# Attention and two expert layers on one core: first weight splits on GpSimd, a condition around the repeated body, and new queue orders

## The chip, the core and the metric

One core of one Trainium2 chip runs the whole program. The metric is device time in microseconds (us) of one execution, smaller is better. The kernel before takes 460.74 us, the median of three runs (460.49 to 464.29).

## What is computed

Three layers follow one another:

```python
q_rot, k_rot = rotate(q), rotate(k)             # 2 batches, 8 heads, 576 tokens, 64 wide
attn = softmax(q_rot @ k_rot.T / sqrt(64))
x = (attn @ v)                                  # -> (1152 tokens, 512)
h = x @ w_in; x = (h * sigmoid(1.702 * h)) @ w_out       # 512 -> 2048 -> 512
e = argmax(x @ w_gate); g = softmax(x @ w_gate)[e]       # one of 8 experts per token
out = g * (relu(x @ w1[e]) @ w2[e])             # 512 -> 1024 -> 512, at most 288 tokens an expert
```

The weights w_in and w_out arrive as 8-byte floats and are made into 4-byte ones on the chip. To keep the accuracy, each 4-byte operand of a large product is split into a high part that TensorE takes as it is and a low part, the rest, and three products (high by high, high by low, low by high) are summed.

## The kernel before, in words

**Attention** works on 8 pairs of heads. For one pair, nine tiles of 128 rows go through the same steps, each a method of `Attention`: `rope` and `start` (rotation of keys and queries, lines 434 and 436), `scores` (TensorE, lines 450 and 461), `least` (VectorE, 473), `exps` (ScalarE, 485), `turn` (transposes by TensorE, 501), `turned` (copies out of PSUM by ScalarE or VectorE, 382 and 383), `rest`, `sums`, `spread` and `placed` for the leftover rows and the row sums, `inverse` (538, 541), `weighted` (TensorE, 576), `divided` (580), and `halved`, which writes the high and low part of the result into `xt` (383 and 591). The function `plan` gives every step of every pair a time out of a table (`FIRST` for pair 0, `SECOND` for pair 1, `LAST` for pair 7, `ORDER` for the others; a unit is a ninth of a pair) and sorts them. `run` issues them in that order, and `pin` chains the instructions of each engine in it, so a table fixes the order of every engine's queue within attention, not the times themselves. `ENGINES` and `LAST_ENGINES` say which engine does a copy.

**The first layer** is `Experts.first`, called for 480, 384 and 288 tokens in turn. For each of 16 slices of the weights, `halves` splits a slice: ScalarE writes the high part (line 744), VectorE the low part (745), into a ring `hl` of four places. `hidden` multiplies (TensorE, 758), `gated` applies the gated function (ScalarE 793 and 794, VectorE 795), and `ffn` multiplies again two slices later (TensorE, 784). In the first call the slices are also made out of 8-byte numbers: `Weights.units` gives, for each slice, two loads (SyncE, 647) and two cuts of three VectorE instructions each (657, 658, 659). The first four slices (`EARLY`) are loaded and cut inside attention, as the events named `spare` of `plan`; the other twelve are issued by `get` and lie where the scheduler puts them. The scheduler also mixes the instructions of the first layer with the end of attention, where data and space allow it.

Space in SBUF is handed out pool by pool, like a stack. The ring `hl` lies where attention kept `turns`, `qk` and `warm` (pool `at_keys`), so its first write waits for the last pair's last scores.

**The second layer** is routed by `route` (rows are sent to a table in memory by GpSimd, 959), fetched by `gather` (1031, 1036), multiplied in `second` and `few`, and sent out by GpSimd (`send`, 1081). Items beyond the four fixed ones run in a loop with a trip count read on the chip; in these inputs there are none, so its body runs zero times:

```python
n = nc.values_load(self.etab[0:1, ITEMS:ITEMS + 1], min_val=4, max_val=ITEMS)
with tc.For_i(4, n, 1) as i:
```

Of the kernel before, what the change touches and what calls it, by code (L numbers as in the profile page):

```python
# [9 lines left out]
F32 = mybir.dt.float32  # L10
# [15 lines left out]
P = 128  # L26
# [19 lines left out]
    (-117.147, 0, 0, CUT, "vector"),  # L46
    (-104.32, 1, 0, P, "vector"),
    (-93.539, 0, CUT, WIDTH, "vector"),
    (-70.102, 1, P, 2 * P, "vector"),
    (-63.518, 1, 2 * P, WIDTH, "gpsimd"),  # L50
# [3 lines left out]
    "rope1": "vector",  # L54
    "t0": "scalar",
    "t1": "vector",
    "t2": "scalar",
    "t3": "vector",
# [4 lines left out]
    "t8": "scalar",  # L63
    "twice": "gpsimd",
    "rr0": "gpsimd",
    "rr1": "gpsimd",
# [4 lines left out]
    "rest_pick0": "scalar",  # L71
# [11 lines left out]
    "t2": "vector",  # L83
# [7 lines left out]
    "rr0": "scalar",  # L91
    "rr1": "scalar",
    "rest0": "vector",
    "rest1": "scalar",
    "sums0": "scalar",
    "sums1": "scalar",
    "rest_pick0": "vector",
    "rest_pick1": "vector",
    "sums_pick0": "scalar",
    "sums_pick1": "scalar",  # L100
    "hix0": "scalar",
    "hix1": "scalar",
    "lox0": "vector",
# [3 lines left out]
RING = 4  # L107
BANKS = 4
# [7 lines left out]
    "scores": (-5.379, 0.0, -5.357, 0.0, -6.652, -5.845, 0.0, -5.773, 0.0),  # L116
    "least": (-4.474, -4.977, -5.096, -5.338, -5.786, -4.946, -5.929, -4.499, -5.286),
    "exps": (-4.007, -2.826, -3.155, -4.498, -4.52, -4.577, -3.986, -3.964, -4.374),
    "turn": (1.18, -0.002, 1.073, 0.066, 0.278, 0.016, -1.338, -2.497, -3.627),
    "turned": (1.29, 1.428, 2.134, 0.802, 0.53, 0.02, 1.733, -2.198, -1.851),  # L120
    "twice": 2.069,
    "rest": (4.203, 7.954),
    "rest_placed": (4.344, 8.225),
    "inverse": (0.431, 5.697),
    "spread": (4.518, 7.776),
    "sums": (8.547, 11.796),
    "sums_placed": (8.668, 11.978),
    "weighted": ((5.82, 5.83, 6.247, 7.416, 7.558), (8.943, 9.276, 9.72, 11.863, 11.866)),
    "divided": (9.825, 12.617),
    "halved": ((10.838, 13.114), (14.097, 16.936)),  # L130
    "rope": (-14.244, -14.237, -11.208, -14.485, -14.198, -8.14),
    "load": (-23.726, -22.572),
    "load_v": -1.934,
    "spare": (58.904, 2.443),
}
FIRST = {
    "scores": (-73.792, 0.0, -59.267, 0.0, -30.868, -18.807, 0.0, -14.272, 0.0),
    "least": (-66.526, -68.104, -48.52, -41.921, -19.608, -13.489, -14.156, -13.209, -13.952),
    "exps": (-48.59, -64.421, -33.102, -36.449, -17.654, -10.259, -11.532, -11.371, -8.342),
    "turn": (-47.159, -45.687, -14.692, -22.644, -11.218, -8.976, -9.913, -7.426, -8.299),  # L140
    "turned": (-34.39, -24.662, -12.818, -6.58, -8.825, -5.338, -6.898, -5.868, -6.252),
    "twice": -11.395,
    "rest": (-10.966, 1.724),
    "rest_placed": (-7.234, 2.438),
    "inverse": (-4.857, 4.371),
    "spread": (3.041, 7.264),
    "sums": (4.504, 7.484),
    "sums_placed": (4.832, 8.961),
    "weighted": ((-2.669, -1.615, 2.832, 4.428, 5.729), (3.158, 4.024, 5.6, 10.857, 10.98)),
    "divided": (6.612, 11.82),  # L150
    "halved": ((8.342, 14.847), (13.13, 19.618)),
    "load_v": -73.006,
# [6 lines left out]
    "turned": (-0.511, -2.93, 2.06, 0.063, 0.948, 2.183, -0.623, 0.18, -0.429),  # L159
    "twice": -2.399,  # L160
    "rest": (3.666, 7.876),
    "rest_placed": (4.094, 8.323),
    "inverse": (-1.23, 5.28),
    "spread": (1.497, 6.761),
    "sums": (8.477, 10.839),
# [1082 lines left out]
```

## Time and profile before

| | us |
|---|---|
| median of 3 runs | 460.74 |
| the profiled execution | 461.19 |
| its span, first to last instruction | 459.4 |
| around the span | 1.8 |

In the profile, PE is the matmuls of TensorE, PEld its weight loads, DVE is VectorE, ACT ScalarE, POOL GpSimd, SP SyncE. A row of a table of windows gives the length of the stretch, then the busy time of each engine with its number of instructions in brackets. A line such as L758 is a line of the kernel. In a timeline the first number is the start, the second the time it took, and square brackets give the idle time before and what ended it. The granted clock of TensorE is 0.994 of 2.4 GHz over the span.

### The profile page before, as it was taken

How to read it: one execution, taken by the hardware profiler on the slowest of the kernel's cores; microseconds unless marked ns; L12 is line 12 of the kernel's file. 1: busy time of each engine (PE TensorE's matmuls, PEld its weight loads, DVE VectorE, ACT ScalarE, POOL GpSimd, SP SyncE). 2: the span in 40 equal slices, each digit the busy share in tenths (PEclk: the TensorE clock that was granted, in tenths of full speed). 3: DMA queues.
4: the chain of work that ended last, by engine and by line, in shares of the span. 5: the costliest groups of instructions: out<-in, count | busy, mean ns of one | idle time of the engine just before them, and what ended most of it. 6: DMA issues, size and time to landing. Idle time of an engine off the chain costs nothing.

```text
span 459.4 us, 9065 instructions
## 1 busy us (share of the span) xinstructions
PE 436.6 (95%) x3380; PEld 373.4 (81%) x3380; DVE 309.7 (67%) x693; ACT 266.0 (58%) x558; POOL 123.9 (27%) x130
## 2 busy tenths in 40 slices
PE   7899999999988999999999999999999999999991
PEld 3556666666565878788999999999999999999980
DVE  5866866677968889997355344457846697765670
ACT  1788888888858252445453445475566455464560
POOL 1589877983210000000000000000526033701020
PEclk9999999999999999999999999999999999999997
DMA  8614421331315756550011600001175446874510
GB/s 279 235 71 145 144 72 75 144 122 30 139 53 177 257 165 245 216 188 1 0 36 34 224 0 1 0 27 46 6 271 182 145 139 186 247 260 157 185 51 16
DMA packets 20319, 57.11 MB, mean 124 GB/s; under 512 B 3749, under 2 KB 5957, under 8 KB 20272
## 3 DMA queue, kind: packets, MB, share of 16 engines
q1 hardware_dynamic: 17584, 52.09, 33.4%
q0 software_dynamic: 1728, 3.62, 2.6%
q10 hardware_dynamic: 960, 0.79, 0.5%
q8 instruction: 28, 0.46, 0.4%
q14 instruction: 19, 0.16, 0.1%
HBM read 49.91 MB, written 6.66 MB: 123 GB/s over the span
## 4 chain that ended last, share of the span: by engine, by line
PE 57%; issue 15%; DVE 10%; DMA 9%; POOL 4%; ACT 3%; SPq 0%; POOLq 0%; DVEq 0%; ACTq 0%
PE h L758 18%; PE y L784 17%; PE t L576 7%; PE s L461 6%; PE t L501 5%; DMA slots<-entry,r_at 2%; DMA raw<-in_w_in 2%; DVE pp L473 2%; POOL slots L959 2%; PE tr L849 2%; POOL out L1081 2%; DVE wf L659 2%; PE s L450 2%; DMA ent<-slots 1%; DVE m L658 1%
## 5 line engine op out<-in xcount | busy, mean ns | idle before, releaser
L758 PE MATMUL h<-xt,hl 128*128 128x288 f32 (+3 forms) x864 | 159.9, 324 | 3.5 <-ACT hl L744 1.4
L758 PEld LDWEIGHTS h<-xt,hl 128*128 128x128 f32 x864 | 135.2, 188 | 11.2 <-ACT hl L744 2.4
L784 PE MATMUL y<-gh,hl 128*128 128x288 f32 (+3 forms) x576 | 123.9, 322 | 0.4 <-ACT gh L794 0.4
L745 DVE TENSOR_TENSOR hl<-wf,hl 128x1024 fp32r<-128x1024 f32 x72 | 87.9, 1224 | 51.3 <-ACT hl L744 51.2
L744 ACT ACTIVATE hl<-wf 128x1024 fp32r<-128x1024 f32 x72 | 76.1, 1059 | 49.6 <-DVE wf L659 26.1
L784 PEld LDWEIGHTS y<-gh,hl 128*128 128x128 f32 x576 | 94.9, 188 | 4.3 <-ACT gh L794 0.8
L784 PE MATMUL y<-gl,hl 128*128 128x288 f32 (+3 forms) x288 | 77.0, 321 | 0.0
L959 POOL DMA_INDIRECT slots<-entry,r_at x12 | 15.0, 1254 | 208.0 <-ACT hl L744 184.3
L793 ACT ACTIVATE g<-h 128x480 f32<-128x480 f32 (+2 forms) x48 | 23.2, 491 | 63.1 <-PE h L758 54.3
L473 DVE TENSOR_SCALAR_CACHE_REDUCE pp<-s 128x576 f32<-128x576 f32 x64 | 45.8, 754 | 16.2 <-PE s L461 15.8
L485 ACT ACTIVATE pp<-pp,nm 128x576 f32<-128x576 f32 x64 | 49.3, 771 | 12.5 <-DVE pp L473 11.8
L784 PEld LDWEIGHTS y<-gl,hl 128*128 128x128 f32 x288 | 50.9, 188 | 1.8
L795 DVE TENSOR_TENSOR gl<-g,gh 128x480 fp32r<-128x480 f32 (+2 forms) x48 | 26.5, 555 | 27.5 <-ACT gh L794 27.2
L434 POOL TENSOR_TENSOR qk<-qk,turns 128x640 f32<-128x640 f32 (+1 forms) x28 | 41.5, 1507 | 9.5 <-DMA qk<-in_qk 9.5
L461 PE MATMUL s<-qk 64*128 64x288 f32 x256 | 40.8, 421 | 3.1 <-DVE pp L473 1.4
L382 ACT ACTIVATE pt<-t 128x512 f32<-128x512 f32 (+1 forms) x65 | 32.8, 538 | 10.4 <-PE t L501 10.3
L576 PE MATMUL t<-pt,vr 128*64 128x288 f32 x256 | 38.3, 419 | 0.1
L501 PEld LDWEIGHTS t<-ident,pp 64*128 64x128 f32 x576 | 23.7, 138 | 16.2 <-issue 4.2
L501 PE MATMUL t<-ident,pp 64*128 64x64 f32 x576 | 28.8, 230 | 2.6 <-ACT pt L382 0.9
L461 PEld LDWEIGHTS s<-qk 64*128 64x128 f32 x256 | 24.0, 188 | 8.3 <-DVE pp L473 2.6
L576 PEld LDWEIGHTS t<-pt,vr 128*64 128x64 f32 x256 | 15.5, 136 | 13.4 <-issue 3.8
L794 ACT ACTIVATE gh<-g 128x480 fp32r<-128x480 f32 (+2 forms) x48 | 24.8, 525 | 1.1
(173 smaller groups left out, 473.6 us busy)
## 6 DMA issues: line engine op xcount, KB each, us to landing
wf<-in_w SPq DMA_DIRECT2D x32, 512.0 KB, 4.5
qk<-in_qk SPq DMA_DIRECT2D x14, 640.0 KB, 5.5
raw<-in_w_in SPq DMA_DIRECT2D x16, 512.0 KB, 4.4
raw<-in_w_out SPq DMA_DIRECT2D x16, 512.0 KB, 3.8
vr<-in_v SPq DMA_DIRECT2D x8, 320.0 KB, 5.0
x<-row SPq DMA_DIRECT2D x12, 192.0 KB, 2.1
out<-zero SPq DMA_DIRECT2D x9, 256.0 KB, 3.0
qk<-in_qk SPq DMA_DIRECT2D x1, 384.0 KB, 4.8
```

The source lines that it names most:

```text
L382: return e.activation(out=out, in_=x, func=AF.Copy)
L434: e.tensor_tensor(out=u, in0=u, in1=self.turns[:, k, ts], op=ALU.mult)
L461: nc.tensor.matmul(both[h][:, n, 0:HALF], q[hs, at:at + P], k[hs, key:key + HALF], start=True, stop=True)
L473: self.nc.vector.tensor_scalar(out=self.room(p, i).rearrange("p (n k) -> p n k", n=2), in0=self.open.pop(("s", p, i))[:, :, 0:HALF], scala ...
L485: self.nc.scalar.activation(out=x, in_=x, func=AF.Exp, scale=-1.0, bias=self.nm[p % 2][:, i:i + 1], accum_out=self.sum[p % 2][:, i:i + 1],)
L501: self.nc.tensor.transpose(banks[b][:, at:at + 64], x[bs], self.ident[bs, bs])
L576: self.nc.tensor.matmul(o[h * 64:h * 64 + 64], x, y, start=j < 2, stop=j > 7)
L744: nc.scalar.activation(out=hl[:, 0], in_=t, func=AF.Copy)
L745: self.last = nc.vector.tensor_tensor(out=hl[:, 1], in0=t, in1=hl[:, 0].bitcast(F32), op=ALU.subtract).ins
L758: self.nc.tensor.matmul(h, u, v, start=m == 0, stop=m == len(ops) - 1)
L784: nc.tensor.matmul(y[j][:, 0:w], u, v, start=f == LAG and m == 0, stop=f == n + LAG - 1 and m == 2)
L795: nc.vector.tensor_tensor(out=gl, in0=g, in1=gh.bitcast(F32), op=ALU.subtract)
```

## The change

1. **Tables and engines.** All five `START` times, every entry of `ORDER`, `FIRST`, `SECOND` and `LAST` and the pace of the early weights (`spare`) are new. In pair 1 both rotations go to GpSimd (the second was VectorE's). In pairs 0 to 6 the copies `t0`, `t2`, `t8` and `rest_pick0` go to VectorE, `t1`, `t3`, `twice`, `rr0` and `rr1` to ScalarE. In pair 7 `rr0` and `lox0` go to GpSimd, `rest1`, `sums1`, both `sums_pick` and both `hix` to VectorE, `t2`, `rest0` and both `rest_pick` to ScalarE.
2. **Space.** `turns` and the `qk` of the pairs that are not the last lie in a pool of their own, `at_odd`; `warm` moves to `at_sums`. The ring becomes two tiles of two places each. The first of them lies in the space of `at_odd`.
3. **Splits.** The first two slices are split by GpSimd, both parts, placed in its queue after its last instruction for pairs 0 to 6.
4. **Order.** The first VectorE instruction of every cut of the twelve later slices is put behind VectorE's last instruction of attention. It is an order within the queue, not a semaphore.
5. **Function table.** After the last `exps` a one-column Gelu on `warm` is issued on ScalarE.
6. **Loop.** The loop stands inside a condition, and its iterations are synchronised in another way.

```diff
     "rope0": "gpsimd",
-    "rope1": "vector",
+    "rope1": "gpsimd",
...
+FIRST_CUTS = 2
...
-    "spare": (58.904, 2.443),
+    "spare": (53.608, 3.254),
...
 LAST = {
...
-    "exps": (-2.224, -5.239, -3.759, -4.874, -3.323, -3.213, -2.722, -3.427, -3.232),
+    "exps": (2.776, -2.966, -2.927, -3.517, -2.774, 2.401, 6.256, 52.03, 36.27),
...
-    "halved": ((78.406, 94.851), (98.733, 141.7)),
+    "halved": ((174.91, 208.013), (237.477, 240.964)),
...
-        self.turns, = some(keys, 1, "turns", 2, WIDTH + 64)
-        self.qk = some(keys, 3, "qk", 4, WIDTH)
-        self.warm = keys.tile([P, 512], BF16, name="warm")
+        last = (B * NPAIR - 1) % 3
+        qk = {k: odd.tile([P, 4, WIDTH], F32, name=f"qk{k}") for k in range(3) if k != last}
+        self.turns, = some(odd, 1, "turns", 2, WIDTH + 64)
+        qk[last] = keys.tile([P, 4, WIDTH], F32, name=f"qk{last}")
+        self.qk = [qk[k] for k in range(3)]
+        self.warm = sums.tile([P, 512], BF16, name="warm")
...
+    def ready(self):
+        self.nc.scalar.activation(out=self.warm[:, 0:1], in_=self.warm[:, 1:2], func=AF.Gelu_apprx_sigmoid)
+
     def run(self, spare):
-        for _, _, f, args in plan(len(spare)):
+        events = plan(len(spare))
+        tail = max(k for k, e in enumerate(events) if e[2] == "exps")
+        for k, (_, _, f, args) in enumerate(events):
             self.pin((lambda: spare[args[0]]()) if f == "spare" else (lambda: getattr(self, f)(*args)))
+            if f != "spare" and f != "start" and args[0] < B * NPAIR - 1:
+                self.calm = dict(self.last)
+            if k == tail:
+                self.pin(self.ready)
...
-            v.tensor_scalar(out=m, in0=top, scalar1=3, scalar2=0x3FFFFFF8, op0=left, op1=both)
+            ins = v.tensor_scalar(out=m, in0=top, scalar1=3, scalar2=0x3FFFFFF8, op0=left, op1=both)
+            if not early:
+                self.tc.add_manual_dep(ins.ins, self.after[ins.ins.engine], self.order, reason="order")
...
-        self.ring = pool("hl", 1).tile([P, RING, 2, 2 * DM], F32R, name="hl")
+        rings = [pool(f"ring{i}", 1) for i in range(RING // 2)]
+        self.ring = [ring.tile([P, 2, 2, 2 * DM], F32R, name=f"hl{i}") for i, ring in enumerate(rings)]
...
     def halves(self, t):
         nc = self.nc
-        hl = self.ring[:, self.cuts % RING]
+        hl = self.slot(self.cuts)
         self.cuts += 1
+        if self.cuts <= FIRST_CUTS:
+            ins = nc.gpsimd.tensor_copy(out=hl[:, 0], in_=t)
+            self.tc.add_manual_dep(ins.ins, self.weights.calm[ins.ins.engine], self.weights.order, reason="order")
+            self.last = nc.gpsimd.tensor_tensor(out=hl[:, 1], in0=t, in1=hl[:, 0].bitcast(F32), op=ALU.subtract).ins
+            return hl
...
-        with tc.For_i(4, n, 1) as i:
+        with tc.If(n > 4, label="more"), tc.For_i(4, n, 1, iteration_sync="staggered") as i:
```

## Rows read from the trace of the kernel before

**Rows 1.** The page's first part: busy time, share of the span, instructions

```profile
PE 436.6 (95%) x3380; PEld 373.4 (81%) x3380; DVE 309.7 (67%) x693; ACT 266.0 (58%) x558; POOL 123.9 (27%) x130
```

**Rows 2.** Windows: the start of attention, and one pair in mid-attention

```profile
7.40:13.50 6.10, 3.84 (x35) 2.12 (x35) 4.25 (x13) 1.96 (x5) 3.40 (x4) 1.00 0.99 364
13.50:20.00 6.50, 5.71 (x51) 3.72 (x52) 6.07 (x13) 4.45 (x13) 4.36 (x4) 1.00 0.53 218
...
87.64:102.46 14.82, 14.70 (x169) 9.63 (x169) 9.82 (x27) 12.91 (x38) 12.20 (x15) 1.00 0.27 96
```

**Rows 3.** Windows: the end of attention and the first layer's first call

```profile
117.20:122.00 4.80, 4.29 (x34) 2.52 (x34) 4.66 (x11) 3.61 (x12) 0.56 (x1) 1.00 0.55 204
122.00:127.00 5.00, 4.51 (x49) 2.77 (x45) 4.93 (x14) 4.54 (x9) 1.22 (x2) 1.00 0.45 144
...
133.40:138.00 4.60, 3.86 (x62) 2.63 (x64) 4.08 (x10) 2.72 (x6) 0.00 (x0) 1.00 0.14 26
138.00:143.40 5.40, 4.43 (x40) 2.36 (x36) 3.59 (x9) 4.78 (x12) 0.52 (x1) 1.00 0.50 175
143.40:148.00 4.60, 3.42 (x15) 2.67 (x16) 4.53 (x9) 3.40 (x8) 0.00 (x0) 1.00 0.50 143
...
168.00:173.00 5.00, 4.45 (x21) 3.37 (x20) 4.16 (x9) 4.11 (x7) 0.00 (x0) 1.00 0.85 255
...
183.00:188.00 5.00, 4.41 (x20) 3.21 (x19) 4.97 (x9) 2.12 (x3) 0.00 (x0) 1.00 0.63 211
188.00:230.00 42.00, 42.00 (x201) 37.01 (x200) 30.89 (x47) 20.40 (x31) 0.00 (x0) 1.00 0.24 88
```

**Rows 4.** Timeline, 123 to 150 us: splits, cuts and the function table

```profile
123.00 0.80 POOL L591 TENSOR_TENSOR xt<-x,xt 128x288 fp32r<-128x288 f32 x1
...
125.18 2.00 ACT L744 ACTIVATE hl<-wf 128x1024 fp32r<-128x1024 f32 x2
...
126.84 2.35 DVE L745 TENSOR_TENSOR hl<-wf,hl 128x1024 fp32r<-128x1024 f32 x2
...
141.49 1.28 ACT L793 ACT_TABLE_LOAD   x1
...
143.41 2.87 PE L758 MATMUL h<-xt,hl 128*128 128x480 f32 x12 [0.98 <-ACT g L793]
...
148.65 0.82 DVE L591 TENSOR_TENSOR xt<-x,xt 128x288 fp32r<-128x288 f32 x2
...
149.74 0.43 DVE L657 TENSOR_SCALAR m<-raw 128x512 uint32<-128x512 uint32 x1 [0.27 <-DMA raw<-in_w_out]
```

**Rows 5.** Groups by line and form: one cut, GpSimd's copy and product

```profile
L659 DVE SCALAR_TENSOR_TENSOR wf<-raw,m 128x512 uint32<-128x512 uint32 x32 | 21.7, 688 | 0.4
L658 DVE SCALAR_TENSOR_TENSOR m<-raw,m 128x512 uint32<-128x512 uint32 x32 | 21.6, 688 | 0.4
...
L657 DVE TENSOR_SCALAR m<-raw 128x512 uint32<-128x512 uint32 x32 | 13.4, 434 | 3.3 <-DMA raw<-in_w_in 2.5 <-DMA raw<-in_w_out 0.6
...
L434 POOL TENSOR_TENSOR qk<-qk,turns 128x640 f32<-128x640 f32 x26 | 39.5, 1547 | 0.0
...
L383 POOL CAST xt<-x 128x288 fp32r<-128x288 f32 x14 | 6.0, 427 | 24.6 <-DVE x L580 24.6
```

**Rows 6.** Timeline: VectorE instructions alone (first) and while GpSimd is busy

```profile
22.32 0.17 DVE L538 TENSOR_SCALAR r<-sum 128x5 f32<-128x5 f32 x1
...
33.66 1.54 POOL L436 TENSOR_TENSOR qk<-qk 128x640 f32<-128x640 f32 x1
...
33.80 1.44 DVE L538 TENSOR_SCALAR r<-sum 128x5 f32<-128x5 f32 x1
```

**Rows 7.** Lines 1081, 1214 and 1244: the last send, the loop, the end

```profile
450.60 0.92 POOL out L1081
...
L1214 PEldq COMPARE_BRANCH  x3: 97/193/3473, 449.6 to 455.7; - x3
...
L1244 POOLq DRAIN  x3: 40/98/2835, 455.8 to 459.1; - x3
```

More of the change, by code (lines that the diff above doesn't have):

```diff
@@ L115 @@
 ORDER = {
[L116 to L133, printed above, removed]
-    "spare": (58.904, 2.443),
+    "scores": (-4.413, 0.0, -4.685, 0.0, -5.375, -4.985, 0.0, -5.165, 0.0),
@@ new lines @@
+    "least": (-3.487, -4.225, -3.923, -4.811, -4.904, -3.433, -5.329, -3.798, -4.32),
+    "exps": (-1.948, -2.637, -3.071, -3.662, -3.273, -1.522, -5.268, -3.308, -3.022),
+    "turn": (1.398, 0.616, 1.713, 0.722, 0.882, 1.025, 0.122, -1.094, -2.4),
+    "turned": (3.851, 0.986, 2.562, 1.284, 1.172, 2.145, 0.545, -0.648, -1.889),
+    "twice": 2.526,
+    "rest": (4.699, 6.75),
+    "rest_placed": (5.113, 7.136),
+    "inverse": (2.173, 9.057),
+    "spread": (6.734, 9.488),
+    "sums": (8.236, 11.015),
@@ L139 @@
[L139 to L149, printed above, removed]
@@ L153 @@
+    "twice": -49.183,
+    "rest": (-42.616, -5.295),
+    "rest_placed": (-33.016, -4.106),
+    "inverse": (-41.977, -4.125),
+    "spread": (-16.569, 1.114),
+    "sums": (-3.694, 4.045),
+    "sums_placed": (-1.282, 6.4),
+    "weighted": ((-12.987, -11.674, -9.633, -7.799, -5.103), (-1.829, 0.864, 3.446, 11.377, 11.593)),
+    "divided": (1.671, 11.932),
+    "halved": ((6.659, 14.31), (17.243, 17.375)),
+    "load_v": -214.704,
 }
 SECOND = {
-    "scores": (-12.787, 0.0, -9.717, 0.0, -9.413, -8.663, 0.0, -8.683, 0.0),
@@ L156 @@
-    "least": (-9.47, -11.138, -8.686, -8.968, -9.228, -8.145, -8.463, -5.311, -6.783),
-    "exps": (-3.824, -9.626, -8.612, -8.417, -8.597, -7.661, -6.941, -4.067, -6.228),
-    "turn": (-2.95, -4.149, 0.795, -0.711, 0.463, -0.018, -0.85, -1.529, -2.326),
[L159 to L165, printed above, removed]
@@ L191 @@
-    "load": (-18.498, -19.788),
-    "load_v": -5.658,
+    "scores": (-5.261, 0.0, -4.682, 0.0, -4.739, -2.873, 0.0, 0.586, 0.0),
+    "least": (-3.737, -4.264, -3.23, -3.549, -3.367, -1.246, -2.088, 1.812, 0.274),
+    "exps": (2.776, -2.966, -2.927, -3.517, -2.774, 2.401, 6.256, 52.03, 36.27),
+    "turn": (3.579, 2.705, 19.261, 19.661, 2.797, 27.454, 25.12, 70.301, 61.619),
+    "turned": (24.628, 21.175, 29.147, 28.362, 15.548, 32.767, 70.661, 74.799, 90.187),
+    "twice": 1.405,
+    "rest": (46.443, 102.682),
@@ L1229, in whole @@
         at.run([u for f in range(EARLY) for u in weights.units(f)])
+    weights.after, weights.calm = at.last, at.calm
     ex = Experts(ctx, tc, d, cst, xt, weights)
```

133 lines of the change are left out of this document (76 added, 57 removed).

## The prediction

> **What bounds the kernel now.** I read the page's busy shares first, then windows over the stages, then the timeline where a window showed idle time. TensorE is busy for 436.6 of 459.4 us [rows 1], so at most some 23 us are to be had, and the question is where TensorE is idle. The windows answer it. In mid-attention a pair takes 14.82 us, of which TensorE is busy 14.70, ScalarE 12.91, GpSimd 12.20 and VectorE 9.82 [rows 2]: TensorE bounds, and all others have room. From 188 us on it is busy without a gap (42.00 of 42.00, last of [rows 3]), so nothing that the change does to later slices can show there. Three places are left.
>
> The start: TensorE idles 6.10 - 3.84 = 2.26 us and then 6.50 - 5.71 = 0.79 us [rows 2], 3.05 together, while VectorE is close to full (6.07 of 6.50). The passage from attention to the first layer: 0.51, 0.49, 0.74, 0.97, 1.18, 0.55 and 0.59 us of idle in the seven short windows of [rows 3], 5.03 together, and here VectorE is the late one (4.66 of 4.80, 4.93 of 5.00, 4.53 of 4.60, 4.97 of 5.00). The end: the last output is sent at 450.60 + 0.92 = 451.5 us, and the final drain starts only at 455.8 and takes 2.84 [rows 7]. A busy TensorE is not TensorE at its peak, so the true idle time may be somewhat more than 8.1 us for the first two; I use the windows.
>
> **The change part by part.** The sum is made against the profiled execution, 461.19 us, which is 0.45 above the median of 460.74.
>
> *Tables and engines, mid-attention: 0.* Per pair ScalarE gives up three copies and one small one, and takes two copies and three small ones; VectorE takes one copy more; GpSimd gives up three small ones. The busy times of [rows 2] move by under 1 us in 14.82, and TensorE's 14.70 stays the bound. The cover is ScalarE's 1.9 us of room in each pair; if the new order made TensorE wait for a copy, it would cost part of that in each of six pairs. Gain at most the idle 0.12 a pair. I take 0, between -0.5 and +1.5.
>
> *Start of attention: -0.8.* Pair 1's second rotation leaves VectorE, which is full there, for GpSimd, which has 6.50 - 4.36 = 2.1 us free [rows 2]. On GpSimd it costs three products at about 1.55 [rows 5], 4.6 us, so that pair 1's keys and queries are ready about 1 us later than now, while pair 0's `least` on VectorE is freed from some 3 us of work. TensorE is waiting for both. I take a quarter of the 3.05 idle us; -2.5 (nearly all of it) and +2.0 (pair 1's scores late by the excess of 4.6 over the 2.1 free) are the ends. The second `load_v` now stands behind pair 2's loads on SyncE; pair 1 needs it a whole pair later, so it costs nothing.
>
> *Passage to the first layer: -4.0.* Four edits act here.
>
> The early cuts. One cut is 0.43 + 0.69 + 0.69 = 1.81 us of VectorE [rows 5]. Cut j stands at 58.904 + 2.443 j now and at 53.608 + 3.254 j then, so the first moves 5.3 units ahead, the fourth 2.9, and the eighth 0.4 back; a unit is 14.82/9 = 1.65 us, so the first four go 8.7 to 4.7 us ahead. They leave the stretch from 117 to 127 us, where VectorE is full, for pair 6, where VectorE has 5 us free [rows 2]. Two or three of them, 3.6 to 5.4 us, find that room.
>
> The splits. The first two slices now cost ScalarE 2.00 and VectorE 2.35 us at 125 to 129 us [rows 4], and both go. GpSimd takes them at 427 x 1024/288 = 1.5 us for a copy and 1547 x 1024/640 = 2.5 for a product, scaled from [rows 5]: 4.0 a slice, 8.0 in all. They stand behind GpSimd's last instruction for pair 6, which ends at 123.0 + 0.8 [rows 4], so the first high part is there at 125.3, the first low at 127.8, the second at 129.3 and 131.8. The first product now starts at 127 us in the same place, so TensorE loses nothing if attention fills a microsecond or two. That they may start before the last pair's scores are over is what the new pool is for; the second half of the ring still waits.
>
> The function table. The load of 1.28 us at 141.49 stands right before the first gated function, and TensorE's wait of 0.98 ends on that function [rows 4]. Moved behind the last `exps`, it falls where ScalarE is idle (2.72 busy of 4.60 between 133.4 and 138, [rows 3]). It costs ScalarE the same 1.28 plus a one-column operation, ahead of copies of the last pair. I take 0.98 as gained, 0 if the gated function is then late for another reason.
>
> The Trainium skill, page "ScalarE: Activation LUTs", section "What ACT_TABLE_LOAD costs", puts a drain of some 1.38 us beside the load, 2.66 in all. Here the first function starts at the load's end; by that page this term would be about 1.4 us larger.
>
> The order for the later weights. Attention's last VectorE instruction ends at 148.65 + 0.82 = 149.47, and the first cut of a later slice starts at 149.74 [rows 4]. The order is thus what happens already and costs nothing in place. Behind the ordered cut in VectorE's queue stand that slice's other two instructions and its split, for which ScalarE and then TensorE wait; so if attention's last instruction moves, all twelve slices move with it, for better or worse.
>
> Summed, 3.6 to 5.4 us of cuts and 2.35 of splits leave VectorE's full stretch, and 0.98 of a wait goes; but only 5.03 us of idle are there. I take 4.0, four fifths: more leaves VectorE than is idle, but the second slice's split is ready later than today. The ends are -5.5 (all, and a little of what windows hide) and +6 (the second rival).
>
> *Loop: -0.7.* Between the send's end at 451.5 and the drain at 455.8 lie the landing of the last rows and the loop's own waits and branches [rows 7]. No row splits a skipped condition from a skipped loop. If the loop's waits are jumped over, up to 2 us go; if the condition adds a jump whose target has to be fetched, the nearest row is TensorE's branch of 3.47 [rows 7], which now lies beside the landing. I take -0.7, close to the small branches of that row (0.1 to 0.2), with ends -2.0 and +3.5.
>
> Sum: 461.19 - 0.8 - 4.0 - 0.7 = 455.7; less 0.45 for the median, 455.2.
>
> **The rivals.**
>
> *VectorE is given back what it was spared (about 459.5).* While GpSimd runs a 1.54 us product, a small VectorE operation from SBUF to SBUF takes 1.44 us instead of 0.17 [rows 6]: it waits for the other's end. GpSimd's 8.0 us of splits now fall on 124 to 132 us, where the last early cuts stand, all from SBUF to SBUF. If half of the 8.0 is lost to VectorE, that is 4.0, more than the 2.35 it was spared, and of the 4.0 and the rest about 1.5 is left: 459 to 460. For it: GpSimd is idle there today, so the meeting is new, as is pair 1's extra rotation. Against it: four cuts leave that stretch, and VectorE's work on scores comes from PSUM.
>
> That is also what the Trainium skill says, page "Advanced Engine Details and Errata", section "VectorE Performance Modes": the second VectorE port of SBUF is shared with GpSimd, and the two block one another. By that rule, and [rows 6] agree, this rival would be the forecast.
>
> *The later weights starve TensorE (about 466).* The new `LAST` puts the last pair's ends far behind everything else (`halved` at up to 241 units instead of 142). If the scheduler lets the first layer's products go ahead of them, attention's last VectorE instruction comes later, and with it every later cut. A slice on TensorE is 24 products, at most twice 2.87 = 5.7 us [rows 4]; at 143.4 three and a half of the four early slices are undone in products and sums together, some 17 us, which lasts to about 160. The fifth slice is ready two cuts and a split after attention's last: 3.6 + 1.0 + 1.2 = 5.8 us. So it decides from 160 - 5.8 = 154, 5 us later than today; beyond that each microsecond costs one. At 164 it costs 10, less the gains before it, 5 us slower. For it: nothing but these numbers holds the tail, and they are large. Against it: they only order attention's own instructions, and TensorE idles today while it waits for them.
>
> *The tables don't carry over (about 460.7).* The idle time is moved about and not filled.
>
> **How the numbers follow.** A measurement of this kernel tells about 1% from no change, 4.6 us: faster means below 456.1. The forecast has 0.56, of which 0.06 ends above that line; its own range is 450 to 457.5, more of it below 455.2 than above, since windows hide some idle time. The port rival has 0.17, the carry-over rival 0.10, starvation 0.17. So faster 0.50, same 0.06 + 0.17 + 0.10 = 0.33, slower 0.17. The range over all cases is 449.5 (460.7 less 3.0 of the start, 5.5 of the passage, 2.0 of the loop and some hidden idle time) to 463.5 (a little into starvation).
>
> **What would show it.** Windows over 7 to 28 us and 117 to 188 us with less idle TensorE, about 2.2 and 1.5 us instead of 3.05 and 5.03; the first slice's split on GpSimd from about 124 us; no table load just ahead of the first gated function; stretch from 188 us on unchanged but earlier by some 4 us. The port rival shows as 657 to 659 taking over 1 us beside GpSimd's splits. Starvation shows as the first later cut after 155 us, with TensorE waiting for 744 and 745. The forecast is wrong if mid-attention pairs take over 15 us, or if the drain starts later after the last send than the 4.3 us of today.

## The result, and the profile after

The kernel after takes 453.89 us (median of 4 runs, 453.46 to 455.43) where the kernel before takes 460.85 (4 runs on the same chip): a ratio of 0.9845, with a 95% interval from 0.9809 to 0.9881. Two later sets of runs timed the kernel after again, each beside the kernel before on the same chip, and gave 0.9890 [0.9847, 0.9932] and 0.9862 [0.9836, 0.9888]. So it is faster by 1.1 to 1.6%, 5 to 7 us. Forecast were 5.5 us, 461.19 to 455.7 in profiled executions. The first profiled execution of the kernel after takes 453.87, 7.3 less than the one before; its span is 452.2 us instead of 459.4.

I read the windows first, the same stretches as in [rows 2] and [rows 3] (length, then busy PE, PEld, DVE, ACT, POOL, granted clock, DMA share, GB/s). The kernel after:

```profile
7.40:13.50 6.10, 4.97 (x30) 2.78 (x31) 4.92 (x15) 2.40 (x7) 3.91 (x4) 1.00 1.00 390
13.50:20.00 6.50, 5.27 (x64) 3.59 (x64) 5.34 (x12) 4.91 (x15) 6.42 (x5) 1.00 0.48 193
87.64:102.46 14.82, 14.46 (x168) 9.72 (x166) 10.31 (x28) 12.98 (x38) 10.28 (x10) 1.00 0.09 26
117.20:122.00 4.80, 4.80 (x39) 2.52 (x37) 4.66 (x10) 3.67 (x14) 0.00 (x0) 1.00 0.54 175
122.00:127.00 5.00, 3.71 (x69) 2.87 (x65) 4.93 (x14) 4.79 (x11) 3.63 (x5) 1.00 0.47 147
127.00:133.40 6.40, 6.09 (x44) 3.07 (x44) 6.33 (x4) 6.11 (x15) 5.55 (x3) 0.73 0.13 50
133.40:188.00 54.60, 54.59 (x265) 45.03 (x265) 48.99 (x96) 22.14 (x33) 4.08 (x4) 1.00 0.58 196
...
188.00:230.00 42.00, 42.00 (x209) 37.60 (x208) 28.97 (x46) 20.62 (x31) 0.00 (x0) 1.00 0.19 63
```

The last but one row takes several stretches of [rows 3] together. The kernel before in it:

```profile
133.40:188.00 54.60, 50.57 (x289) 39.96 (x290) 48.60 (x96) 26.44 (x47) 0.52 (x1) 1.00 0.58 196
```

TensorE's idle time in the first two windows is 1.13 and 1.23 us (2.26 and 0.79 before); in the pair of mid-attention it is 0.36 instead of 0.12; from 117 to 133.4 us it is 0, 1.29 and 0.31 (1.07 together before, so it grew), and from there to 188 us 0.01 instead of 4.03. In this profile the marks that the prediction set for idle time are met: 2.36 us where it said about 2.2, 1.60 in the passage where it said 1.5. The two later profiles of the same kernel show 3.13 and 2.61 us up to 20 us, where the kernel before has 3.05, and 2.23 and 2.59 in the passage; in the first profile TensorE's clock was halved for 3.41 us there (the row with 0.73), which shows as busy time. No table load stands ahead of the gated function, and TensorE is full from 188 us on, as said. The first slice's split starts on GpSimd at 126.57 and not at about 124.

What TensorE waited for between 117 and 190 us says the same by releaser (line waited for: us in total, times, longest). The kernel before:

```profile
PE h L758 <- ACT hl L744: 1.4, 2, 1.2
PE h L758 <- ACT g L793: 1.0, 1, 1.0
...
PE h L758 <- DVE hl L745: 0.6, 1, 0.6
...
```

and the kernel after, which has these two and no more:

```profile
PE t L506 <- ACT pt L387: 1.2, 3, 0.8
PE t L506 <- DVE x L585: 0.3, 1, 0.3
```

The waits for splits (744, 745) and for the gated function (793) are gone. The new one is for a copy of transposed exponentials, which ScalarE makes late since its high part of the third slice stands ahead of it in the queue.

The timeline of the kernel after between 125 and 147 us shows the moved work and its price (start, duration, engine, line; numbers in brackets are idle time before):

```profile
126.57 3.22 POOL L768 CAST hl<-wf 128x1024 fp32r<-128x1024 f32 x2
126.84 2.05 DVE L773 TENSOR_TENSOR hl<-wf,hl 128x1024 fp32r<-128x1024 f32 x1
...
128.81 1.52 DVE L677 SCALAR_TENSOR_TENSOR m<-raw,m 128x512 uint32<-128x512 uint32 x1
...
129.76 2.80 POOL L770 TENSOR_TENSOR hl<-wf,hl 128x1024 fp32r<-128x1024 f32 x1
...
130.20 1.28 ACT L610 ACT_TABLE_LOAD   x1
130.37 2.74 DVE L678 SCALAR_TENSOR_TENSOR wf<-raw,m 128x512 uint32<-128x512 uint32 x1
...
132.90 0.71 PE L786 MATMUL h<-xt,hl 128*128 128x480 f32 x2
...
136.15 3.17 DVE L773 TENSOR_TENSOR hl<-wf,hl 128x1024 fp32r<-128x1024 f32 x1 [0.17 <-ACT hl L772]
...
138.28 0.57 ACT L821 ACTIVATE g<-h 128x480 f32<-128x480 f32 x1 [1.87 <-POOL hl L770]
```

Lines 768 and 770 are GpSimd's two splits. Beside them four VectorE instructions take 2.05, 1.52, 2.74 and 3.17 us; the median of their lines in this profile is 1.23, 0.69, 0.69 and 1.23 (lines 773, 677, 678, 773). That is 9.48 less 3.84, 5.6 us lost by VectorE. The first product of the first layer is at 132.90 and not at 127.07, yet TensorE idles less over the passage. GpSimd's second product, which the lines leave out, runs only from 135.86 to 138.24: a copy of the last pair that the change gave to GpSimd (`rr0`) stands ahead of it and waits 2.95 us for VectorE. The prediction had the second slice's low part ready at 131.8.

The end, lines 1109 (send) and 1273 (end), to be set against [rows 7]; queue instructions with count, shortest/median/longest in ns, first and last start:

```profile
L1109 POOL DMA_INDIRECT out<-row,ent x9: 918/943/1502, 390.7 to 446.4; - x9
...
L1273 SPq EVENT_SEMAPHORE  x14: 17/28/848, 448.4 to 452.1; - x14
...
L1273 POOLq DRAIN  x3: 44/103/2835, 448.5 to 451.9; - x3
```

The last send starts at 446.35 instead of 450.60. From there to the drain of 2.84 us are 2.2 us instead of 5.2, and SyncE's longest wait, 0.85 us for the landing of the last rows, lies beside the drain. From the last send to the end of the span are 5.84 us, where there were 8.81.

Three long windows sum it up. Idle TensorE is the length less PE; the third profile of the kernel after (its clock was full in all three) is the better one to compare. The kernel before:

```profile
7.40:58.00 50.60, 45.60 (x485) 29.37 (x485) 38.26 (x96) 38.61 (x106) 39.01 (x38) 1.00 0.45 164
58.00:117.20 59.20, 58.70 (x672) 38.39 (x672) 40.03 (x112) 51.63 (x148) 42.62 (x50) 1.00 0.25 86
117.20:188.00 70.80, 65.70 (x409) 50.28 (x408) 61.36 (x122) 37.86 (x76) 3.53 (x6) 1.00 0.54 181
```

The kernel after, third profile:

```profile
7.40:58.00 50.60, 47.77 (x503) 30.75 (x504) 39.30 (x101) 41.14 (x115) 42.34 (x34) 1.00 0.47 164
58.00:117.20 59.20, 57.95 (x675) 39.63 (x672) 46.13 (x126) 51.35 (x149) 38.10 (x36) 1.00 0.31 105
117.20:188.00 70.80, 68.21 (x411) 52.87 (x411) 64.69 (x121) 36.84 (x72) 13.18 (x11) 1.00 0.52 176
```

The start gains 5.00 - 2.83 = 2.2 us, mid-attention loses 1.25 - 0.50 = 0.75, the passage gains 5.10 - 2.59 = 2.5, the end 8.81 - 5.84 = 3.0: 6.95 in all. That is a sum over stages. This profile's span is 455.1 us, only 4.3 less than the 459.4 before, since the stretch from the last cut to the last send, which these rows do not cover, is 2.7 us longer in it; in the first profile that stretch is as long as before, and all of its 7.2 us arrive.

### The profile page after: what moved, and what is told of

It is laid out like the page before. It is cut to its first block, busy times and chain, and to the rows that moved or that the text cites. A ratio compares the mean times of both kernels' runs of the same rounds, so it can differ in the third digit from the quotient of the medians.

```text
span 452.2 us, 8892 instructions
## 1 busy us (share of the span) xinstructions
PE 436.8 (97%) x3380; PEld 375.6 (83%) x3380; DVE 315.7 (70%) x704; ACT 265.2 (59%) x560; POOL 132.4 (29%) x118
## 4 chain that ended last, share of the span: by engine, by line
PE 69%; issue 13%; POOL 6%; DVE 6%; DMA 5%; ACT 1%; POOLq 0%; DVEq 0%
PE h L786 24%; PE y L812 22%; PE t L581 8%; PE s L466 5%; PE t L506 5%; PE tr L877 2%; POOL qk L439 2%; POOL out L1109 2%; DMA slots<-entry,r_at 2%; PE s L455 2%; DVE pp L478 1%; POOL slots L987 1%; DVE m L677 1%; DMA turns<-in_turns 1%; DMA qk<-in_qk 1%
## 5 line engine op out<-in xcount | busy, mean ns | idle before, releaser
L772 ACT ACTIVATE hl<-wf 128x1024 fp32r<-128x1024 f32 x70 | 74.1, 1059 | 49.3 <-DVE wf L678 24.5
L987 POOL DMA_INDIRECT slots<-entry,r_at x12 | 15.0, 1252 | 202.5 <-ACT hl L772 178.8
L478 DVE TENSOR_SCALAR_CACHE_REDUCE pp<-s 128x576 f32<-128x576 f32 x64 | 45.8, 754 | 14.7 <-PE s L466 14.3
L439 POOL TENSOR_TENSOR qk<-qk,turns 128x640 f32<-128x640 f32 (+1 forms) x30 | 44.9, 1513 | 16.4 <-DMA qk<-in_qk 16.4
L581 PE MATMUL t<-pt,vr 128*64 128x288 f32 x256 | 39.5, 430 | 0.1
L506 PEld LDWEIGHTS t<-ident,pp 64*128 64x128 f32 x576 | 26.0, 139 | 14.3 <-issue 3.9
L387 ACT ACTIVATE pt<-t 128x512 f32<-128x512 f32 (+1 forms) x59 | 29.9, 539 | 6.8 <-PE t L506 6.5
L506 PE MATMUL t<-ident,pp 64*128 64x64 f32 x576 | 30.3, 229 | 2.4 <-ACT pt L387 1.2
L581 PEld LDWEIGHTS t<-pt,vr 128*64 128x64 f32 x256 | 16.4, 140 | 13.1 <-issue 4.1
```

The source lines that it names most:

```text
L387: return e.activation(out=out, in_=x, func=AF.Copy)
L439: e.tensor_tensor(out=u, in0=u, in1=self.turns[:, k, ts], op=ALU.mult)
L478: self.nc.vector.tensor_scalar(out=self.room(p, i).rearrange("p (n k) -> p n k", n=2), in0=self.open.pop(("s", p, i))[:, :, 0:HALF], scala ...
L506: self.nc.tensor.transpose(banks[b][:, at:at + 64], x[bs], self.ident[bs, bs])
L581: self.nc.tensor.matmul(o[h * 64:h * 64 + 64], x, y, start=j < 2, stop=j > 7)
L772: nc.scalar.activation(out=hl[:, 0], in_=t, func=AF.Copy)
```

## The experiments

For each profile the table gives idle TensorE in those three stretches, and two measures that don't hang on fixed times: the **reach**, from the second pair's scores for its tile 4 (line 450; 27.65 us before) to the first instruction of the last cut (208.40 before), and the **end**, from the last send to the end of the span. A star marks a stretch in which the granted clock fell to 1.2 GHz for a while; idle time there says less, and the reach is used. Each row is one profile. The last two rows are the same kernel, and their reach differs by 2.2 us, so a difference of that size can come without an edit.

| kernel | idle 7.4 to 58 | 58 to 117 | 117 to 188 | reach | end | ratio to before, 95% |
|---|---|---|---|---|---|---|
| before | 5.00 | 0.50 | 5.10 | 180.8 | 8.81 | 1 |
| after, first | 2.57 | 1.25 | 1.61* | 177.2 | 5.84 | 0.9845 [0.9809, 0.9881] |
| after, second | 3.36 | 1.25 | 2.23 | 176.9 | 5.83 | 0.9890 [0.9847, 0.9932] |
| after, third | 2.83 | 1.25 | 2.59 | 177.2 | 5.83 | 0.9862 [0.9836, 0.9888] |
| before, condition | 4.82 | 0.51 | 5.34 | 181.0 | 7.31 | 0.9967 [0.9935, 1.0000] |
| before, staggered | 4.51* | 0.47 | 5.06 | 180.6 | 9.00 | 1.0006 [0.9988, 1.0024] |
| before, new tables | 3.49 | 1.25 | 4.46 | 179.4 | 8.87 | 0.9967 [0.9932, 1.0003] |
| after, old tables | 4.92 | 0.48 | 4.09* | 180.6 | 5.62 | 0.9942 [0.9919, 0.9965] |
| after, no GpSimd splits | 3.07* | 2.25 | 4.63 | 181.3 | 5.85 | 0.9898 [0.9854, 0.9942] |
| after, old pace | 3.27* | 3.74* | 6.74* | 187.0 | 5.83 | none |
| after, no order | 2.64 | 1.24 | 1.75* | 177.5 | 5.83 | 0.9883 [0.9828, 0.9938] |
| after, no early Gelu | 3.31* | 1.25 | 2.63 | 177.1 | 5.84 | 0.9867 [0.9843, 0.9890] |
| after, third split late | 3.43* | 1.24 | 4.23 | 178.8 | 5.83 | 0.9820 [0.9786, 0.9854] |
| the same again | 3.42 | 1.23 | 2.38 | 176.6 | 5.83 | 0.9853 [0.9837, 0.9870] |

### The condition alone

```diff
-        with tc.For_i(4, n, 1) as i:
+        with tc.If(n > 4, label="more"), tc.For_i(4, n, 1) as i:
```

> The kernel before with only the condition put around its loop (the loop itself unchanged). Theory A: about 3.0 us of the gain come from the end alone. In the profile of the changed kernel the last send is issued 4.25 us earlier but the span ends 7.2 us earlier, because GpSimd's final drain of 2.84 us starts right after its branch instead of after the landing of the last rows and the loop's waits. Then this run is 457.9 us (-3.0), with 5.8 us from the last send's issue to the end instead of 8.8. Rival (the step of the prediction): a skipped condition saves only 0.7, so 460.1 us. Second rival: it is the other way of synchronising iterations that does it, then no change, 460.8.

The end fell by 1.5 us, half of what the change gives and between the two theories. Lines 1214 and 1244 of this kernel:

```profile
L1214 POOLq EVENT_SEMAPHORE  x4: 17/43/1528, 451.5 to 451.8; - x4
...
L1244 POOLq DRAIN  x3: 40/103/2835, 454.2 to 457.6; - x3
```

GpSimd still waits 1.53 us for the landing of the last rows before the drain, which then starts 3.7 us after the last send (450.56). Before, it was 5.2 (455.77 less 450.60). What is skipped is the loop's own meeting of the engines.

### The staggered loop alone

```diff
-        with tc.For_i(4, n, 1) as i:
+        with tc.For_i(4, n, 1, iteration_sync="staggered") as i:
```

> The kernel before with its unchanged loop staggered, without the condition around it. Theory A (the condition and the staggering each take one half of the 2.97 us that the end lost; the condition alone took 8.81 us from the last send to the end of the span down to 7.31): from the last send to the end 7.3 to 7.4 us, a drain on GpSimd that still starts behind the loop's waits; the profiled execution about 1.5 us below 461.2 at a last send near 450.6. Rival (staggering does something only inside a condition that skips the loop): 8.8 us from the last send to the end, as before.

The rival is right: 9.00 us, nothing gained. Lines 1214 and 1244:

```profile
L1214 PEldq COMPARE_BRANCH  x2: 101/1760/3419, 453.9 to 454.0; - x2
...
L1244 POOLq DRAIN  x3: 40/98/2835, 458.1 to 461.4; - x3
```

GpSimd no longer waits for the landing ahead of the loop, but the engines meet once before the loop and once behind it, and the second meeting waits for TensorE's branch of 3.42 us out of the empty loop. Under a condition this branch starts earlier (445.1 us in the kernel after, ahead of the last send) and nothing waits for it. So the condition gives 1.5 us by itself, and the staggering another 1.5, but only inside the condition.

### The new tables alone

```diff
-    (-117.147, 0, 0, CUT, "vector"),
+    (-196.795, 0, 0, CUT, "vector"),
...
-    "spare": (58.904, 2.443),
+    "spare": (53.608, 3.254),
...
```

All of part 1 of the change goes into the kernel before, and nothing else.

> The kernel before with the new tables and engines (start, pair orders, pace of the early weights, who copies), and nothing else of the change. Theory A: the tables carry most of the 4.25 us that the last send is earlier: about 2 us at the start of attention (TensorE's waits up to 58 us) and most of the 2.1 us between 165 and 190 us, as the later cuts start at 146 instead of 149.7 us: 457 us. Rival: the tables fit only the kernel whose first splits are on GpSimd; then the start's 2 us stay but the passage gains nothing or loses: 459 to 461 us.

The rival is right. The start gains nearly as in the kernel after (5.00 to 3.49 us idle), mid-attention loses its 0.75, and the passage keeps 4.46 of its 5.10. Its windows, cuts and TensorE's longest wait there:

```profile
138.00:143.40 5.40, 4.69 (x34) 2.94 (x31) 2.59 (x8) 3.60 (x7) 0.53 (x1) 1.00 0.00 0
143.40:148.00 4.60, 4.60 (x24) 3.53 (x23) 3.06 (x9) 1.53 (x4) 1.16 (x1) 1.00 0.00 2
```

```profile
138.42 0.43 DVE L657 TENSOR_SCALAR m<-raw 128x512 uint32<-128x512 uint32 x1 [1.74 <-DMA raw<-in_w_out]
...
148.66 0.69 DVE L659 SCALAR_TENSOR_TENSOR wf<-raw,m 128x512 uint32<-128x512 uint32 x1
...
162.48 0.70 PE L758 MATMUL h<-xt,hl 128*128 128x480 f32 x2 [1.76 <-ACT hl L744]
```

The first cut of a later slice begins at 138.42, and its third instruction comes at 148.66. VectorE is half idle and the loads stand still (DMA share 0.00) in between. At 162.48 TensorE waits 1.76 us for a later slice's split. That the half-done cut causes this wait is not shown: the run without the order, below, has such a cut too (begun at 139.28, third instruction at 146.48), with loads that stand still until 148 us, and TensorE has no such wait there.

### The splits without the tables

```diff
-    "spare": (53.608, 3.254),
+    "spare": (58.904, 2.443),
...
```

The reverse: the kernel after with all of part 1 undone.

> The kernel after with all six tables of the kernel before (engines, due times, spare): only the splits on GpSimd, the later weights' wait for attention's last instructions and the loop are new. Theory A (the parts add up): start and middle of attention as before, TensorE's lag 31.1 us at 117 us, then the passage of the kernel after (7.9 us more by 188 us, against 10.8 before) to 39.0; with 3.0 us from the end of the kernel that is 461.2 - 2.8 - 3.0 = 455.4 for the profiled execution, a ratio to the kernel before of about 0.988. Rival (tables and splits fit only each other, as the new tables alone gained nothing before the first layer): the first later cut after 150 us, TensorE's lag at 188 us 41.5 or more, so only the 3.0 us of the end are left: 458.2, ratio about 0.9935.

The ratio of 0.9942 is that of the rival. The loop's 3 us alone would give 0.9935; reach 180.6, as before. (The rival's cut after 150 us was not seen; it starts at 148.49. The lag of which the expectation speaks is not used here; idle time and reach stand in its place.) The timeline shows why the splits bring nothing here:

```profile
128.47 2.22 POOL L768 CAST hl<-wf 128x1024 fp32r<-128x1024 f32 x2
128.54 1.24 DVE L674 TENSOR_SCALAR m<-raw 128x512 uint32<-128x512 uint32 x1
129.82 1.41 DVE L677 SCALAR_TENSOR_TENSOR m<-raw,m 128x512 uint32<-128x512 uint32 x1
130.65 2.80 POOL L770 TENSOR_TENSOR hl<-wf,hl 128x1024 fp32r<-128x1024 f32 x1
131.26 2.74 DVE L678 SCALAR_TENSOR_TENSOR wf<-raw,m 128x512 uint32<-128x512 uint32 x1
...
136.00 1.06 ACT L772 ACTIVATE hl<-wf 128x1024 fp32r<-128x1024 f32 x1 [3.72 <-issue]
...
137.58 0.50 PE L506 MATMUL t<-ident,rr 64*128 64x64 f32 x4 [1.88 <-ACT ptr L387]
...
139.41 2.85 DVE L678 SCALAR_TENSOR_TENSOR wf<-raw,m 128x512 uint32<-128x512 uint32 x1
```

VectorE loses as much as in the kernel after (0.43 and 0.69 taken off, 5.7 us), but all of it on early cuts: they run as late as in the kernel before, so when GpSimd begins, 1.9 us later than in the kernel after, four of the eight are still to be done. In the kernel after the first cut starts at 102.13 instead of 114.17, and two are left then (126.49 and 133.14). One of the four is the third slice's second cut. It ends at 135.92, and only then can ScalarE write that slice's high part (136.00, after 3.72 us of idle time, for which the profile names no releaser); the copies behind it in ScalarE's queue come late, and TensorE waits 1.88 us for one. In the kernel after that cut ends at 125.22, before GpSimd begins. The first product comes at 135.0. Tables and splits gain little alone (1.3 and 0.2 us of reach), and some 3.5 together.

### No splits on GpSimd

```diff
-FIRST_CUTS = 2
+FIRST_CUTS = 0
```

> The changed kernel with no split on GpSimd: the first two slices are split by ScalarE and VectorE as in the kernel before, all else stays. Theory A: GpSimd's splits give nothing or little, since VectorE loses to them what it is spared: 126.84 to 139 us hold four VectorE instructions with 5.6 us more than their usual time beside GpSimd's copies and products, against 2.35 us of splits spared. Then this run is 453 to 454.5 us, equal within the measurement, and TensorE's clock does not fall at 128 us. Rival: the splits are what lets the passage fill; then 456 us or more (+2 and up), with TensorE waiting for ScalarE and VectorE at 125 to 130 us.

Without GpSimd's splits the collisions are gone too, and still the reach is 181.3, 4 us more than in the three profiles of the kernel after. The ratios don't tell these kernels apart, and two other things are in the 4 us. The profile is of the slowest of the four runs (463.48 us, median 459.43), with the clock down for 6.83 us at the start; the kernel in the table's last two rows had 2.2 us more reach in its profile with such a fall than in the one without. And the edit moves more than the engine: ScalarE's high part of the first slice now stands in mid-attention, ahead of its data.

```profile
111.28 1.06 ACT L772 ACTIVATE hl<-wf 128x1024 fp32r<-128x1024 f32 x1 [1.45 <-DVE wf L678]
```

TensorE waits 0.61 and 0.41 us for copies behind it, which is the 2.25 us of idle time instead of 1.25 ahead of 117 us. So that the splits pay for their collisions is likely but not shown; they are worth something between nothing and 4 us.

### The old pace of the early weights

```diff
-    "spare": (53.608, 3.254),
+    "spare": (58.904, 2.443),
```

> The changed kernel with the old pace of the early weights (58.904, 2.443), all else stays. Theory A: moving the early cuts ahead into pair 6 is the main part of the passage's gain, because VectorE is late from 117 to 135 us: with the old pace two to three cuts (3.6 to 5.4 us) come back into the full stretch and the later cuts start 2 to 3 us later: 455.5 to 457 us. Rival: VectorE has idle time between 138 and 146 us in the changed kernel that takes them up: 453.9 us, no change.

This took 468.37 us in the median (462.61 to 472.41), too spread for a ratio, and 5.7 us more than the kernel before in the median. What TensorE waited for between 102 and 190 us:

```profile
PE t L581 <- ACT pt L387: 5.0, 1, 5.0
...
```

The first cut starts at 112.32 us instead of 102.13, and ScalarE sits idle for 3.81 us ahead of its high part of the third slice:

```profile
138.26 1.06 ACT L772 ACTIVATE hl<-wf 128x1024 fp32r<-128x1024 f32 x1 [3.81 <-POOL hl L768]
```

The releaser shown is GpSimd's copies, which end at 137.36; that slice's second cut, which takes 3.78 us beside them instead of 1.87, ends at 137.90 and fits better. It is the wait of the run with the old tables again. The copies of the exponentials stand behind it in ScalarE's queue, and TensorE waits 5.0 us for one of them. The first later cut starts at 157.82. My own expectation of a small loss was wrong by some 10 us. Part of them may be the clock's: its mean over the four runs sinks from 0.989 at 462.61 us to 0.974 at 472.41, and the profile has three falls, the longest of 6.83 us at 115.4.

### No order for the later weights

```diff
-            if not early:
+            if not early and False:
```

> The changed kernel without the order of the later cuts behind attention's last. Only VectorE's queue changes, by one cut: its first two instructions come at about 139 us instead of 146, the third stays behind attention's last, since the weight's place is free only then. Theory A: the order matters, because that half-done cut holds its raw buffer and so the next load; the run with the tables alone, which has no such order, shows it (first cut instruction at 138.4, third at 148.7, no transfers between 138 and 148, then TensorE idle for some 2.2 us between 148 and 168): +1 to +2 us against the changed kernel. Rival: VectorE is idle there anyway, so no change within 0.5 us.

The rival is right. The first later cut starts 6.7 us earlier:

```profile
139.28 0.43 DVE L674 TENSOR_SCALAR m<-raw 128x512 uint32<-128x512 uint32 x1
```

Reach 177.5 and the ratio are those of the kernel after. The order costs and brings nothing.

### No early Gelu

```diff
-            if k == tail:
+            if k == tail and False:
```

> The changed kernel without the one-column Gelu after the last exps: the function table is loaded right before the first gated function again, 1.28 us. Theory A: 0 to 0.5 us, because in the changed kernel the first gated function starts at 138.28 after ScalarE sat idle for 1.87 us, waiting for the first slice's last product, and TensorE has other slices and attention work then. The rival is the step of the prediction, 0.98 us: 1.0 us slower, with TensorE waiting for the gated function.

Theory A is right. The table's load is back ahead of the first gated function, and TensorE waits 0.45 us for it:

```profile
139.26 1.28 ACT L821 ACT_TABLE_LOAD   x1 [0.69 <-PE t L506]
140.55 0.57 ACT L821 ACTIVATE g<-h 128x480 f32<-128x480 f32 x1
...
141.17 3.31 PE L786 MATMUL h<-xt,hl 128*128 128x480 f32 x14 [0.45 <-ACT g L821]
```

Reach 177.1 and ratio are unchanged: at most these 0.45 us hang on it.

### The third slice's high part later on ScalarE, and the yardstick

The wait for `pt` that is left in the passage suggested one more step: ScalarE's high part of the third slice behind its last exponentials.

```diff
-        nc.scalar.activation(out=hl[:, 0], in_=t, func=AF.Copy)
+        ins = nc.scalar.activation(out=hl[:, 0], in_=t, func=AF.Copy)
+        self.cuts > FIRST_CUTS + 1 or self.tc.add_manual_dep(ins.ins,
+            self.weights.over[ins.ins.engine], self.weights.order, reason="order")
```

> The changed kernel with ScalarE's copy for the third slice's split put behind the last exps (in the changed kernel it stands at 125.37 us, 1.06 us ahead of the copies of the last pair's transposes, and TensorE waits 0.79 and 0.22 us for those at 126 to 127.5, just before its clock falls). Theory A: TensorE no longer waits there, the clock doesn't fall at 128, and 1 to 2.5 us are gained over the changed kernel. Rival: the wait only moves, as ScalarE is full at 122 to 133 us (4.79 of 5.00, 6.11 of 6.40): within 0.5 us.

It had the lowest ratio of all, but its profile had the clock down for 6.83 us at the start and a worse passage. So it ran again, with the kernel after beside it:

> The kernel after with ScalarE's half of the third early split ordered behind its last exponentials (as in the run before it of the same kernel, which had the lowest ratio, 0.982, but a profile with a clock fall at the start), beside the kernel after itself in the same call. Theory A (TensorE's wait for the exponentials at 126 us behind that copy is on the path): TensorE's lag grows 0.7 us less from 122 to 133 us and the ratio lies 0.0015 to 0.003 below that of the kernel after. Rival (what is gained there is given back by 138 us, since the copy and the product behind it only come later): no difference between the two that the intervals can tell.

> The kernel after unchanged, as the yardstick of this call: ratio 0.985 to 0.989 to the kernel before, 5.84 us from the last send to the end. Theory A (the clock's falls come by chance): a fall to 1.2 GHz near 14 us or 128 us in some profiles of this same kernel and not in others. Rival (they belong to the kernel's order of work): the fall of 3.41 us at 128 us again, as in the profile of the kernel after, and none at the start.

456.69 and 456.54 us, 0.9853 and 0.9862 with intervals that overlap: no difference, as the rival has it. The wait at 126 us shrinks, and TensorE waits 1.2 us for `pt` at 133.5 instead. The kernel after had been timed a second time before that:

> The changed kernel once more, unchanged, as the yardstick for the three runs beside it (the kernel before took 462.64 in the last set of runs, 460.85 in the first). Both theories expect a ratio of 0.985 to before. What it tells: where TensorE's granted clock falls this time. In the first profile it fell to 1.2 GHz for 3.41 us at 127.9 us. If the fall belongs to this kernel's order of work, it is there again; if it comes by chance, it is elsewhere or gone.

It shows what one profile is worth: the idle time of the start varies from 2.57 to 3.36 us and that of the passage from 1.6 to 2.6 over three profiles of one kernel, while reach stays within 0.3 (none of the three has a clock fall at the start).

## Why the prediction was right, and where it was not

The forecast of 455.2 and the sum of 5.5 us stand against 453.89 and 7.0 in the same set of runs. The time came out near, with the terms in other sizes; by the table below the start and the loop gave 3.7 us more than forecast, the passage and mid-attention 2.25 less. That these cancel in part is luck.

| term | forecast | measured |
|---|---|---|
| start of attention | -0.8 | -2.2 (-1.6 to -2.4 over three profiles) |
| mid-attention | 0 | +0.75 |
| passage to the first layer | -4.0 | -2.5 (-2.9 in another profile, -3.5 in the one with the clock's fall) |
| loop | -0.7 | -3.0 |

**Start.** The direction was right, the place and the cause for the most part were not. VectorE's window did fall from 6.07 to 5.34 busy, and GpSimd's rose to 6.42 of 6.50, full but not late for TensorE. But of the 3.05 idle us up to 20 us, of which the term is a quarter, 2.36, 3.13 and 2.61 are left in the three profiles, and 3.26 with the new tables alone. The gain lies between 20 and 58 us, where I had not looked: 1.96 us of idle before, 0.20 to 0.23 in the three profiles. 1.2 of these were waits for ScalarE's copies of transposed exponentials (line 382), not for VectorE. The new tables alone show this gain (0.23); which of their entries gives it was not tried.

**Mid-attention.** The term was 0 within -0.5 and +1.5, and it is 0.75: the pairs take 15.00 us instead of 14.82 (their scores for tile 4 start at 70.16, 85.17 and 100.17). That the limit I set for "wrong" was 15 shows how close it was. VectorE's busy time rose by 6 us between 58 and 117 us, partly by cuts that moved there. What costs the 0.18 us a pair was not tried.

**Passage.** Here the signs were right and the bookkeeping was not. I summed what leaves VectorE (cuts and splits) against 5.03 us of idle. VectorE's full stretch did not empty either: from 117 to 127 us it is busy for 4.66 of 4.80 and 4.93 of 5.00 us before and after, since later cuts took the place of those that left. What moved is the end of the early cuts, 135.02 instead of 146.31, and TensorE's gain lies behind 133.4 us. The runs show that neither edit counts alone: the tables by themselves gain some 1.3 us of reach and the splits 0.2, both together some 3.5, each by one profile. The traces show a reason: with the new tables the third slice's cuts are over before GpSimd begins, and with the old ones or the old pace they are not, and ScalarE's queue stands still for 3.7 and 3.8 us. The splits began at 126.57 instead of 123.8, since GpSimd's last work for pair 6 ends 2.8 us later in the new order. The first product came 5.8 us later than "in the same place", and "TensorE loses nothing if attention fills a microsecond or two" nearly held, over a longer stretch: its idle time from 117 to 133.4 us grew by 0.5 to 1.0 us over the three profiles. The end of attention, which the forecast left to the scheduler, moved ahead: VectorE's last instruction for it ends at 146.10 instead of 149.47.

**Function table.** The 0.98 us counted as gained were on the path of the kernel before, but are not on that of the kernel after: 0.45 at most. The Trainium skill, page "ScalarE: Activation LUTs", section "What ACT_TABLE_LOAD costs", has a drain beside the load; the traces show none in front of the function: 139.26 + 1.28 = 140.54, and it starts at 140.55.

**Order.** Costed at nothing, and nothing it is.

**Loop.** This term failed, and outside its own ends (-2.0 to +3.5). The step was "if the loop's waits are jumped over, up to 2 us go". I took the landing of the last rows for a fixed time ahead of the drain. But GpSimd can start its drain of 2.84 us while the landing is still under way, and SyncE waits for it meanwhile. That is the second 1.5 us, and only both edits together give it.

**The rivals.** The port rival's mechanism is there, at a higher price than I gave it: 5.6 us over four instructions instead of 4.0, three of them at more than twice their usual time. The Trainium skill, page "SBUF — State Buffer", section "SBUF: two separate sides", says that VectorE with two SBUF inputs and GpSimd lock one another out for a whole instruction; all four are of that kind. The trace agrees: the one of 2.74 us ends at 133.11, 0.55 us after GpSimd's product (132.56), where its line usually takes 0.69 in all. The rival's own sign, 657 to 659 over 1 us, was there too (677 and 678 here, 1.52 and 2.74). But TensorE hardly pays the price, as it has attention's products to do meanwhile: 0.01 to 0.51 us of idle from 133.4 to 188 us in the three profiles. What I missed is that an engine's loss counts only where the next engine is out of work. With the old tables, where the same loss falls on a cut that ScalarE's queue waits for, the rival is nearly the result (0.9942). Starvation did not come: the first later cut starts at 146.02, far from 154. It does come by one line, the old pace, at 157.8 us and 468 us in the median, near the rival's 466, though by another path than its working: ScalarE's queue, not the later weights. That the tables don't carry over holds for the tables alone (0.9967).

**The last step of the path.** Not all the gain arrives in every profile. From the first instruction of the last cut to the last send the kernel before takes 242.2 us, and the three profiles of the kernel after 242.2, 243.3 and 244.9; TensorE idles 0.93 us there before, and 0.95, 1.98 and 2.54 after. The staggered kernel before shows 243.7 and 1.71, so it is not the change alone. In the third profile of the kernel after the longest waits between 340 and 440 us are for ScalarE's relu in the routed layer and for fetched rows:

```profile
PE y L812 <- ACT gh L827: 1.0, 1, 1.0
PE tg L1082 <- DMA got<-x,ent: 0.5, 1, 0.5
```

The second is there in the kernel before too (0.48). Whether the earlier arrival makes the first likelier stays open. It does not order the ratios: the longest stretch, 244.9, belongs to 0.9862 and not to 0.9890.

## What to carry to other kernels

Work moved to an idle engine and the room made for it ahead of time are one edit: here each alone gained little, and a single pair of pacing numbers could cost some 10 us. Price a collision by who runs out of work, and by what stands in a queue behind the instruction that waits for the slowed one, not by how long the slowed one takes. At the end of a kernel look at what the last engine waits for before its drain: a skipped loop can still hold a wait that could lie beside the drain.

## What the hardware showed unasked

The granted clock fell to 1.2 GHz inside the work in some profiles of a kernel and not in others. The kernel after had one fall of 3.41 us at 127.9 in its first profile and none in the two others, with the same waits of TensorE ahead of it (0.3, 0.2, 0.8 and 0.2 us); the run without the order had it in the same place, at 128.3. Other kernels had one of 3.41 or 6.83 us between 13 and 24 us, at 115 or near 139. The kernel after without GpSimd's splits, for instance:

```profile
13.50:20.00 6.50, 5.58 (x23) 3.24 (x25) 1.87 (x5) 2.41 (x7) 6.42 (x6) 0.52 0.50 206
```

TensorE issued 23 products there, where the kernel after issued 64. A fall at the start goes with a late start. In the four profiles in which the first pair's scores for tile 4 come last, at 13.58 to 14.09 us, the clock falls at 13.7 to 16.5; in the ten others, where they come at 12.79 to 13.54, it does not fall so early; one of these has a fall at 20.96. What decides is not shown. A fall at the start delays what is behind it: from those scores to the second pair's it takes 14.1 to 14.3 us without a fall, 15.2 to 15.4 with one of 3.41 us and 16.2 to 16.4 with one of 6.83. The one at 128 us costs nothing that can be seen, as it lies where TensorE waits otherwise (1.11 us idle in that window at the full clock in the third profile, 0.31 at the fallen one in the first), and reach is the same.

TensorE's branch over an empty loop or a skipped condition took 3.32 to 3.86 us in the 14 profiles, where the other engines' took 0.04 to 0.07. It was seen to cost time where the engines meet behind it, in the staggered run.
